# Four shift products of a query block: a turn of four score tiles of their own, or four 32-column tiles beside a block of sums

## Chip, cores and metric

One NeuronCore of a Trainium2 chip. The metric is the device time of one execution in microseconds (us), the median of the runs.

## What is computed

Two rounds of the same two layers on x of 2048 rows by 512 columns, float32. Cut to what matters here (the second layer, a mixer over the rows, is left out):

```python
q = (layernorm(x) @ wq).reshape(1, 2048, 32, 16).transpose(0, 2, 1, 3)
k, v = layernorm(x) @ wk, layernorm(x) @ wv          # one key and value head of 16 for all 32 heads
scores = einsum("bhqd,bkd->bhqk", q, k) * 16 ** -0.5
x = x + (softmax(scores) @ v).transpose(0, 2, 1, 3).reshape(1, 2048, 512) @ wo
```

The kernel takes no maximum of the scores ahead of the exponential. Each query and head gets a shift from a bound: minus 0.515625 times its squared length, times a bound on the keys. It goes into the score product as two more rows. The sums of squares over the 16 columns of a head are the "shift products" of this case.

## The kernel before

**Tiling.** The 2048 queries are four blocks b of 512. A block's 512 query columns are four quarters m of 128 columns (8 heads of 16), and a quarter makes two groups of four heads. So a layer has 32 groups, and a group has 32 score tiles: 16 key tiles by two pairs of heads, 1024 tiles in a layer. `scores` (L906) makes one tile with two matmuls on two halves of the rows into a two-bank PSUM tile `sc` (three of them), and ScalarE writes the exponential to `p` (L922). Some tiles are first copied by VectorE (L920). `sums` (L924) multiplies `p` with values and ones: each float32 product is two matmuls of 32 columns in the trace, and two tiles with j0 = 0 and 2 fill the four 32-column tiles of the array side by side, `acc` (L928). `acc` of a group is one of two PSUM banks, by the group's parity; the other one is the spare bank in which projections are made (`spare`, L946).

**The order of TensorE's work** is written out in turns (L36 to L53), run by `Attention.run` (L988). A positive number k makes k % 10 score tiles (13 means three, the last copied by VectorE), 0 takes the next part (a projection or the like), and a negative number drains so many tiles into sums. The four that matter, with one letter for each:

```python
WHOLE = (13, 0, 0, 13, -4, 13, -4, 13, -4)                  # W, 12 tiles
LONG = (2, 0, 13, -4, 13, -4, 13, 0, 13, -4, 12, -4)        # L, 16 tiles
TINY = (2, 0, 2, -4)                                        # T, 4 tiles
PLAIN = (2, -2)                                             # P, 2 tiles
```

**What is queued.** `Proj.later` (L649) lists the query work that is left when the attention of a layer begins. For a quarter it is a W with two parts of six matmuls, `pq` (L418). After a block's last quarter comes a T with the block's shift products, `shifts` (L548). Layer 0 has 14 quarters and four T, layer 1 has 11 quarters and four T. All must be over before tile 256, and a turn that would cross tile 64 (layer 0), 128 (layer 1) or 256 is replaced by P (L1019 to L1023). A W becomes an L where 14 tiles or more are left in the group being summed and `slack` (L983) is at least 4. That is 256, less the tiles scored, less the sizes of all queued turns, less 48 (before tile 160) or 12. An L doesn't begin with 2, 4 or 32 tiles left in the group, nor a W with 2 (L1026, L1028); a P stands there. Output projections `po` come ahead of the queue once their divisions are done in `mix.step` on VectorE, one or two small steps at a drain. When nothing else is to be had, P follows P up to tile 256.

**A quarter's way.** The second part sets `behind` (L705): at the next drain `put_queries` (L541) rounds `pq` on VectorE (L519), squares it on GpSimd into `sq` (L527), subtracts on VectorE (L531) and stores by SyncE's queue. `shifts` multiplies `sel` (a 0 or -0.515625 matrix, 128 by 32 for each quarter) with `sq` of the four quarters, one after the other into the same 32 PSUM rows (L552). Then VectorE takes the minimum `qmin` (L556) and the copy `c2` (L557), and one DMA writes `c2` (L717). `lowest` (L596) sends `qmin` through DRAM to one row for the check of the bound, `flag` (L611), which the guards at those tiles read. Between the layers `shifts` runs once with two quarters, from L1624. The way in (L1491) makes quarter 0 of layer 0 by itself (L1506).

Of the kernel before, what the change touches and what calls it, by code (L numbers as in the profile page):

```python
# [18 lines left out]
P = 128  # L19
# [30 lines left out]
SHORT = (2, 0, 3, -4, 3, -4)  # L50
TINY = (2, 0, 2, -4)
PLAIN = (2, -2)
# [20 lines left out]
def kernel(  # L73
# [37 lines left out]
    ident = cp.tile([P, P], F32, tag="ident", name="ident")  # L111
    sel = cp.tile([P, ND, H], BF16, tag="sel", name="sel")
    selk = cp.tile([P, 1], BF16, tag="selk", name="selk")
    b1c = cp.tile([P, NF], F32, tag="b1c", name="b1c")
    b2c = cp.tile([P, NKT], F32, tag="b2c", name="b2c")
    qmin = cp.tile([H, NB + 1], F32, tag="qmin", name="qmin")
    k2m = cp.tile([P, NKT], F32, tag="k2m", name="k2m")
# [3 lines left out]
    cd = dp.tile([NB * NG, 4, 2, QB], F32, tag="cd", name="cd")  # L121
    fd = dp.tile([3, H, NB], F32, tag="fd", name="fd")
    hd = [dp.tile([P, ND, 2, QB], F32, tag=f"hd{b}", name=f"hd{b}") for b in range(2)]
# [7 lines left out]
    def f32(ap):  # L131
        return ap.bitcast(F32)
# [6 lines left out]
    def constants():  # L139


        kr = cp.tile([1, 4, P], F32, tag="kr", name="kr")
        half = kr.rearrange("o j (e r) -> o j e r", e=2)
        nc.gpsimd.memset(kr, 0.0)
        nc.gpsimd.memset(kr[:, 1, :], 1.0)
        nc.gpsimd.memset(half[:, 0, :, 2 * R1 + 1 : KR], 1.0)
        nc.gpsimd.memset(half[:, 1, :, 2 * R1 + 1 : KR], -1.0)
        for t in range(3):
            nc.gpsimd.memset(half[:, 2, :, t * R1 : t * R1 + 1], 1.0)
        nc.gpsimd.memset(kr[:, 3, 1:R1], 1.0)  # L150
        pk = bank(0, "pkc")
        for j in range(4):
            nc.tensor.matmul(pk[:, j : j + 1], kr[:, j, :], onerow[:, :1], start=True, stop=True)
        heat(16, bank(1, "pw"))
        nc.gpsimd.memset(vaug[:, :, :, 1], 1.0)
        nc.gpsimd.memset(sel, -SHIFT)
        for m in range(ND):

            nc.gpsimd.affine_select(
                sel[:, m, :], sel[:, m, :], pattern=[[-DH, H]], compare_op=ALU.is_ge,  # L160
                fill=0.0, base=P * m, channel_multiplier=1,
            )
            nc.gpsimd.affine_select(
                sel[:, m, :], sel[:, m, :], pattern=[[DH, H]], compare_op=ALU.is_ge,
                fill=0.0, base=DH - 1 - P * m, channel_multiplier=-1,
            )
        return pk
# [83 lines left out]
    class Proj:  # L251
        def __init__(self, layer, spare=None):
            n = self.l = layer
            self.sq, self.h, self.hT, self.kv, self.y = {}, {}, {}, {}, {}
            self.kk, self.kg, self.pk, self.pq, self.q2, self.st = {}, {}, {}, {}, {}, {}
            self.pt, self.halves = {}, {}

            self.spare, self.half = spare, None
            if spare:
                self.first = pool(f"first{n}", side="right")  # L260

            k = self.keep = pool(f"keep{n}")
            self.wq = k.tile([P, ND, 2, D], F32R, tag="wq", name=f"wq{n}")
            self.c2 = k.tile([H, 2, QB], F32R, tag="c2", name=f"c2_{n}")
            p = self.pool = pool(f"proj{n}")
            self.wkv = p.tile([P, ND * 2, P], F32R, tag="wkv", name=f"wkv{n}")
# [29 lines left out]
        def empty(self, eng=None):  # L296
            nc.vector.memset(f32(self.wkv), 0.0)
            eng = eng or nc.vector
            eng.memset(f32(self.c2), 0.0)
            self.ones = self.pool.tile([P, P], F32, tag="ones", name=f"ones{self.l}")  # L300
            eng.memset(self.ones, -SHIFT)
# [245 lines left out]

        def shifts(self, b, pc=None, parts=range(ND)):  # L548

            pc = (bank2(f"pc{self.l}_{b}")[:, 0, :] if pc is None else pc)[:H, :]  # L550
            for m in parts:
                nc.tensor.matmul(  # L552
                    pc, sel[:, m, :], self.sq.pop((b, m)), start=(m == parts[0]), stop=(m == parts[-1])
                )
            c = b + 1 if b or parts[0] else 0
            nc.vector.tensor_reduce(qmin[:, c : c + 1], pc, axis=AX.X, op=ALU.min)  # L556
            nc.vector.tensor_copy(self.c2[:, 0, :], pc)  # L557
            put_shifts(self.c2, NG * b + 2 * parts[0], NG * b + 2 * parts[-1] + 2, 8 * parts[0])

# [45 lines left out]
        def load_lowest(self, j, k):  # L605

            self.far = sm.tile([1, H, NB - 1], F32, tag="far", bufs=1, name=f"far{self.l}_{j}")
            nc.sync.dma_start(self.far[:, :, :k], fd[j : j + 1, :, :k])
            self.low = k
# [39 lines left out]
        def later(self, att):  # L649

            n, work = self.l, []

# [5 lines left out]

            def rows(b, parts=range(ND)):
                put(TINY, [lambda i: self.shifts(b, bank(i, f"pc{n}_{b}"), parts)])  # L660

            def far(j, lo, hi):
                then(-1, lambda: self.lowest(j, lo, hi))

# [4 lines left out]
            if n == 0:  # L669
                project(0, range(2, ND))  # L670
                then(-1, lambda: (self.first.release(), att.weights()))
                rows(0, range(1, ND))
                far(1, 1, 2)
                for b in range(1, NB):
                    project(b)
                    rows(b)
            else:
                att.weights()
                project(NB - 2, [ND - 1])
                then(-1, lambda: self.fetch(0))  # L680
                rows(NB - 2)
                project(0, range(2, ND))
                then(-1, lambda: (self.fetch(1), att.split_weights(1)))
                rows(0, range(2, ND))
                far(1, 1, 2)
                for b in (NB - 1, 1):
                    project(b)
                    rows(b)
            for j in range(2 - n):
                k = j + (3 if n == 0 else 2)  # L690
                then(k, lambda j=j: att.split_weights(j))
            far(2, 2, NB + 1)
            return work

# [99 lines left out]
    class Attention:  # L794
        def __init__(self, layer):
# [4 lines left out]
            self.spares, self.taken = None, 0  # L800
            self.behind, self.lag, self.pieces = None, LAG, []

# [180 lines left out]
        def slack(self, later):  # L983

            left = 2 * NKT * NG - self.scored - sum(self.size(t) for t, _, _ in later)
            return left - (48 if self.scored < 2 * NKT * 5 else 12)

        def run(self, mix, proj):  # L988
# [10 lines left out]
            while self.scored < total:  # L999
                mix.chores(self)  # L1000
                ahead = min(t for t in guards if t > self.scored)
                known = ahead < guards[-2] or not later
                if ahead < total and self.scored >= ahead - 16 and flagged < ahead and known:
                    flagged = ahead
                    proj.flag(proj.flagged)
                if turn is None:
                    turn = PLAIN
                    self.lag = 2 * LAG if mix.normed and self.scored < total - 16 else LAG
                    if len(self.pend) == self.lag:
                        after, queued = None, bool(later) and not mix.projections  # L1010
                        if queued:
                            turn, parts, after = later[0]
                            if turn is WHOLE and self.to_boundary() >= 14 and self.slack(later) >= 4:
# [17 lines left out]
                for k in turn:  # L1031
                    if k > 0:
                        self.more(mix, k)
                    elif k == 0:
                        if queued and turn is TINY:
                            mix.step(2.0, self)
                        parts.pop(0)(self.spare())
                        if turn is DOUBLE and len(parts) % 2:
                            mix.step(1.0, self)
                        if queued and not parts:  # L1040
                            later.pop(0)
                            if after:
                                after()
                            if not later:
                                proj.close()
                                mix.open()
                    else:
# [4 lines left out]
                        if busy:  # L1052
                            self.behind = None
                            busy()
                        self.drain(-k)
                        mix.chores(self)
# [7 lines left out]
                        elif end:  # L1064
                            mix.step(2.0, self)
                assert self.scored < guards[-2] or not later
                if self.scored in guards[:-1] and self.scored > guarded:
# [423 lines left out]
    def way_in(order, proj):  # L1491
# [13 lines left out]
        def pc():  # L1505
            nc.tensor.matmul(halves("pc", 0)[:H, :], sel[:, 0, :], proj.sq.pop((0, 0)), start=True, stop=True)  # L1506

        def c2():
            nc.scalar.copy(proj.c2[:, 0, :], halves("pc", 0)[:H, :])

        def qmin_():
            nc.vector.tensor_reduce(qmin[:, :1], halves("pc", 0)[:H, :], axis=AX.X, op=ALU.min)

# [213 lines left out]
```

## Time and profile before

| what | value |
|---|---|
| runs | 2510.74, 2510.95, 2515.05 us; median 2510.95 |
| span of the profiled execution | 2509.2 us |
| median less that span (what lies around it) | 1.75 us |
| TensorE busy, granted clock | 2492.8 us, 99%; 0.999 |
| ScalarE, VectorE, GpSimd busy | 2101.7, 1550.9, 148.2 us |

The span runs from the first to the last instruction of the one execution that was profiled; durations below are of it. Starts on TensorE are exact, while ends of matmuls are modelled, so that a block's price is read from its start to the start of the next.

### The profile page before, as it was taken

To read this page: it belongs to the slowest core of one execution; us is meant where nothing else is said; L and a number is where in the kernel's file an instruction comes from. 1 tells how busy PE (TensorE), PEld (TensorE's weight loads), DVE (VectorE), ACT (ScalarE), POOL (GpSimd) and SP (SyncE) were. 2 spreads that over 40 slices of the span, in tenths; PEclk is the share of its full clock that TensorE was granted. 3 is DMA by queue.
4 is the path that set the end of the run, shared out by engine and by line. 5 is a ranking of instruction groups with operands and counts; after the bars stand their busy time and mean duration, and the time that the engine had idled before them with its cause. 6 is when DMAs were issued, how large, how long until landed. Compare 5 with 4: busy or idle time off the path is not lost. (4 is left out here: it accounts for less than half of the span.)

```text
span 2509.2 us, 41946 instructions
## 1 busy us (share of the span) xinstructions
PE 2492.8 (99%) x16158; PEld 1240.5 (49%) x16158; DVE 1550.9 (62%) x2458; ACT 2101.7 (84%) x2344; POOL 148.2 (6%) x235
## 2 busy tenths in 40 slices
PE   8999999999999999999999999999999999999999
PEld 6444344444444444588863443444444444445887
DVE  6566566667766776564445664666677667765522
ACT  6999999999999999653349999999999999995511
POOL 5000000000000000141000000000000000002200
PEclk9999999999999999999999999999999999999999
DMA  3221201111111111144423211111111111102343
GB/s 117 75 66 41 65 28 40 31 42 31 39 31 39 31 40 32 41 112 149 126 61 118 58 48 48 31 39 33 39 31 39 32 43 33 40 26 67 106 125 96
DMA packets 168679, 143.56 MB, mean 57 GB/s; under 512 B 17650, under 2 KB 132368, under 8 KB 167952
## 3 DMA queue, kind: packets, MB, share of 16 engines
q1 hardware_dynamic: 168464, 140.72, 19.0%
q8 instruction: 132, 2.16, 0.4%
q14 instruction: 83, 0.68, 0.1%
HBM read 97.67 MB, written 26.22 MB: 49 GB/s over the span
## 5 line engine op out<-in xcount | busy, mean ns | idle before, releaser
L922 ACT ACTIVATE p<-sc 128x1024 f32<-128x1024 f32 x1444 | 1405.8, 1049 | 62.9 <-PE sc L912 62.2
L920 DVE COPY p<-sc 128x1024 f32<-128x1024 f32 x604 | 739.1, 1224 | 522.3 <-PE sc L912 436.4
L928 PE MATMUL acc<-p,vaug 128*32 128x512 f32 x8192 | 1000.1, 599 | 0.5 <-DVE q L531 0.5
L912 PE MATMUL sc<-qs,kst 51*128 51x512 f32 x4096 | 683.5, 432 | 6.8 <-SPq L630 2.7
L922 ACT ACTIVATE p<-p 128x1024 f32<-128x1024 f32 x604 | 655.9, 1086 | 14.1 <-DVE p L920 9.2
L912 PEld LDWEIGHTS sc<-qs,kst 51*128 51x128 f32 x4096 | 338.3, 184 | 559.5 <-ACT p L922 387.3
L928 PEld LDWEIGHTS acc<-p,vaug 128*32 128x32 f32 x8192 | 219.0, 109 | 489.3 <-issue 472.9
L1458 PE MATMUL py<-u,w 128*128 128x512 f32 x1344 | 307.4, 390 | 0.0
L1458 PEld LDWEIGHTS py<-u,w 128*128 128x128 f32 x1344 | 251.9, 188 | 52.3
L1446 ACT CAST w<-w2r 128x896 fp32r<-128x896 f32 x64 | 60.3, 945 | 184.6 <-PE py L1458 177.3
L1205 PE MATMUL pu<-hb,w 128*128 128x512 f32 x792 | 209.6, 406 | 0.0
L1205 PEld LDWEIGHTS pu<-hb,w 128*128 128x128 f32 x792 | 140.9, 188 | 57.7 <-issue 31.9
L1192 POOL TENSOR_TENSOR w<-w1r,w 128x256 fp32r<-128x256 f32 x86 | 70.0, 822 | 1581.5 <-ACT w L1190 1581.1
L1447 DVE TENSOR_TENSOR w<-w2r,w 128x896 fp32r<-128x896 f32 x64 | 72.0, 1124 | 111.4 <-ACT w L1446 111.2
L848 DVE RECIPROCAL o<-o 128x128 f32<-128x128 f32 x120 | 113.3, 944 | 9.4 <-DMA o<-ev 9.4
L889 PE MATMUL po<-wo,hl 128*128 128x512 f32 x360 | 100.4, 412 | 0.1
L830 DVE COPY ev<-acc 128x512 f32<-128x512 f32 x64 | 43.7, 682 | 62.1 <-PE acc L928 62.1
L418 PE MATMUL pq<-hT,wq 128*128 128x512 f32 x312 | 81.1, 404 | 0.0
L889 PEld LDWEIGHTS po<-wo,hl 128*128 128x128 f32 x360 | 62.6, 188 | 33.9 <-issue 16.0
L1205 PE MATMUL pu_l<-hb,w 128*128 128x512 f32 x336 | 77.1, 389 | 0.0
L1464 DVE SCALAR_TENSOR_TENSOR x<-py,b2c,x 128x512 f32<-128x512 f32 x32 | 24.0, 750 | 81.2 <-PE py L1458 81.2
L1190 ACT CAST w<-w1r 128x256 fp32r<-128x256 f32 x86 | 34.5, 406 | 47.1 <-PE pu_l L1205 14.3
(191 smaller groups left out, 1179.0 us busy)
## 6 DMA issues: line engine op xcount, KB each, us to landing
w1r<-in_B_w_dram SPq DMA_DIRECT2D x224, 128.0 KB
w2r<-in_B_w_dram SPq DMA_DIRECT2D x64, 448.0 KB
qs<-qd SPq DMA_DIRECT2D x384, 64.0 KB
qd<-q SPq DMA_DIRECT2D x64, 256.0 KB
o<-ev SPq DMA_DIRECT2D x128, 128.0 KB
x<-in_A_x_dram SPq DMA_DIRECT2D x16, 256.0 KB
hd<-hT SPq DMA_DIRECT2D x2, 2048.0 KB
out_dram<-x SPq DMA_DIRECT2D x16, 256.0 KB
```

Of the source, the lines that this page charges most:

```text
L418: yield nc.tensor.matmul(out, a, c, start=(k == 0), stop=(k == len(terms) - 1))
L848: nc.vector.reciprocal(o[:, 1, c], o[:, 1, c])
L889: nc.tensor.matmul(po, a, c, start=(k == 0), stop=(k == 3 * len(parts) - 1))
L912: nc.tensor.matmul(sc[:, j, :], kst[kt // 4][rows, kt % 4 * P : (kt % 4 + 1) * P], qs[i % NQ][rows, j0 // 2, :], start=True, stop=True,)
L920: nc.vector.tensor_copy(pt, sc)
L922: nc.scalar.activation(pt, sc, AF.Exp, scale=0.25)
L928: nc.tensor.matmul(self.acc[i][c : c + 32, :], vaug[:, kt].rearrange("p d k -> p (d k)"), pt[:, j, :], start=(kt == 0), stop=(kt == NKT - ...
L1192: eng.tensor_tensor(w[:, 1], raw, f32(w[:, 0]), op=ALU.subtract)
L1205: nc.tensor.matmul(pu, a, c, start=(start and k == 0), stop=(stop and k == 5))
L1446: nc.scalar.copy(w[:, 0], raw)
L1447: nc.vector.tensor_tensor(w[:, 1], raw, f32(w[:, 0]), op=ALU.subtract)
L1458: nc.tensor.matmul(py, a, d, start=(c == 0 and f == 0 and k == 0), stop=(c == 1 and f == NFH - 1 and k == 2),)
```

## The change

The four products go to four 32-column tiles of one bank: `pc` rows 32m to 32m+31 for quarter m, each a product by itself, with one `sel` for all. `qmin` and `c2` therefore have 128 rows, and each quarter's shifts go out by a DMA of its own. T is gone. What it held is a "tail" of the queue's entry before it, emitted just ahead of a drain once that entry has no part left, if the drain isn't the one that emits `put_queries` and doesn't cross the group's end. Until a tail is out no further turn is taken from the queue. Layer 0's first tail makes quarter 0 again (its `sq` is kept). The core of the diff:

```diff
-TINY = (2, 0, 2, -4)
-    sel = cp.tile([P, ND, H], BF16, tag="sel", name="sel")
+    sel = cp.tile([P, H], BF16, tag="sel", name="sel")
-    qmin = cp.tile([H, NB + 1], F32, tag="qmin", name="qmin")
+    qmin = cp.tile([P, NB + 1], F32, tag="qmin", name="qmin")
-    fd = dp.tile([3, H, NB], F32, tag="fd", name="fd")
+    fd = dp.tile([3, P, NB], F32, tag="fd", name="fd")
...
             eng.memset(f32(self.c2), 0.0)
+            eng.memset(qmin, 0.0)
...
+        def shifts(self, b, pc=None, parts=range(ND), new=0):
+
+            pc = bank2(f"pc{self.l}_{b}")[:, 0, :] if pc is None else pc
             for m in parts:
                 nc.tensor.matmul(
-                    pc, sel[:, m, :], self.sq.pop((b, m)), start=(m == parts[0]), stop=(m == parts[-1])
+                    pc[H * m : H * m + H, :], sel, self.sq.pop((b, m)), start=True, stop=True,
+                    skip_group_check=True,
                 )
-            put_shifts(self.c2, NG * b + 2 * parts[0], NG * b + 2 * parts[-1] + 2, 8 * parts[0])
+            rows = slice(H * parts[0], H * parts[-1] + H)
+            c = b + 1 if b or ND - 1 in parts else 0
+            nc.vector.tensor_reduce(qmin[rows, c : c + 1], pc[rows, :], axis=AX.X, op=ALU.min)
+            nc.vector.tensor_copy(self.c2[rows, 0, :], pc[rows, :])
+            for m in parts[new:]:
+                put_shifts(self.c2, NG * b + 2 * m, NG * b + 2 * m + 2, H * m)
...
-            def rows(b, parts=range(ND)):
-                put(TINY, [lambda i: self.shifts(b, bank(i, f"pc{n}_{b}"), parts)])
+            def rows(b, parts=range(ND), new=0):
+                tails[len(work) - 1] = [lambda i: self.shifts(b, bank(i, f"pc{n}_{b}"), parts, new)]
...
-                        if queued and turn is TINY:
-                            mix.step(2.0, self)
...
+                        elif self.tail and not parts and self.to_boundary() >= -k > 0:
+                            spare = self.spare()
+                            for part in self.tail:
+                                part(spare)
+                            self.tail = None
+                            if not later:
+                                proj.close()
+                                mix.open()
                         self.drain(-k)
```

In the way in, `sel` takes two `affine_select` on GpSimd in place of eight. The row that `lowest` loads takes 8 of each quarter's 32 rows of `fd`.

## Rows read from the trace of the kernel before

**Rows 1.** The page, part 1: busy us, share of the span, instructions.
```profile
PE 2492.8 (99%) x16158; PEld 1240.5 (49%) x16158; DVE 1550.9 (62%) x2458; ACT 2101.7 (84%) x2344; POOL 148.2 (6%) x235
```
**Rows 2.** Windows: stretch, then busy us of PE, PEld, DVE, ACT, POOL; clock, DMA.
```profile
57.00:291.00 234.00, 233.18 (x1617) 99.05 (x1609) 136.63 (x176) 219.28 (x235) 14.56 (x14) 1.00 0.22 59
...
1527.00:1545.00 18.00, 18.00 (x120) 5.65 (x118) 2.78 (x11) 18.00 (x21) 0.00 (x0) 1.00 0.18 52
```
**Rows 3.** Timeline of PE, a W and a T of layer 0: start us, us, what.
```profile
136.50 0.96 PE L912 MATMUL sc<-qs,kst 51*128 51x512 f32 x6
...
143.09 0.96 PE L912 MATMUL sc<-qs,kst 51*128 51x512 f32 x6
143.98 1.92 PE L928 MATMUL acc<-p,vaug 128*32 128x512 f32 x16
...
148.58 0.73 PE L912 MATMUL sc<-qs,kst 51*128 51x512 f32 x4
149.25 1.04 PE L552 MATMUL pc<-sq,sel 128*32 128x512 bf16 x4
150.22 0.95 PE L912 MATMUL sc<-qs,kst 51*128 51x512 f32 x4
...
152.95 0.97 PE L912 MATMUL sc<-qs,kst 51*128 51x512 f32 x6
```
**Rows 4.** Timeline of PE, the first T of layer 0 (three products).
```profile
86.17 0.73 PE L912 MATMUL sc<-qs,kst 51*128 51x512 f32 x4
86.83 0.82 PE L552 MATMUL pc<-sq,sel 128*32 128x512 bf16 x3
87.58 0.88 PE L912 MATMUL sc<-qs,kst 51*128 51x512 f32 x4
...
90.25 0.73 PE L912 MATMUL sc<-qs,kst 51*128 51x512 f32 x4
```
**Rows 5.** Timeline of PE in layer 1: an L and the T behind it.
```profile
1308.99 0.73 PE L912 MATMUL sc<-qs,kst 51*128 51x512 f32 x4
...
1322.64 1.92 PE L928 MATMUL acc<-p,vaug 128*32 128x512 f32 x16
1324.50 0.73 PE L912 MATMUL sc<-qs,kst 51*128 51x512 f32 x4
...
1328.65 0.73 PE L912 MATMUL sc<-qs,kst 51*128 51x512 f32 x4
```
**Rows 6.** Timeline of PE in layer 1: the last T, the first P behind it and a later one.
```profile
1520.88 0.73 PE L912 MATMUL sc<-qs,kst 51*128 51x512 f32 x4
...
1525.13 0.73 PE L912 MATMUL sc<-qs,kst 51*128 51x512 f32 x4
...
1526.79 0.73 PE L912 MATMUL sc<-qs,kst 51*128 51x512 f32 x4
...
1530.54 0.73 PE L912 MATMUL sc<-qs,kst 51*128 51x512 f32 x4
...
1532.37 0.73 PE L912 MATMUL sc<-qs,kst 51*128 51x512 f32 x4
```
**Rows 7.** Timelines of DVE and POOL behind the pq of Rows 3.
```profile
142.59 0.68 DVE L519 CAST q<-pq 128x512 fp32r<-128x512 f32 x1
...
143.41 1.04 POOL L527 TENSOR_TENSOR sq<-q 128x512 bf16<-128x512 f32 x1 [11.07 <-DVE q L519]
```
**Rows 8.** Timeline of POOL behind the pq of Rows 5.
```profile
1322.20 1.04 POOL L527 TENSOR_TENSOR sq<-q 128x512 bf16<-128x512 f32 x1 [21.96 <-DVE q L519]
```
**Rows 9.** Tile pc, the minimum: engine, operation, count, ns min/median/max, first and last start.
```profile
L556 DVE TENSOR_REDUCE qmin<-pc x9: 669/679/679, 87.7 to 1523.9; 32x1 f32<-32x512 f32 x9
```
**Rows 10.** Timeline of SP behind the last T of layer 0.
```profile
288.20 0.34 SPq L717 DMA_DIRECT2D cd<-c  x1
```
**Rows 11.** Timelines of PE and POOL in the way in.
```profile
3.23 1.86 PE L153 MATMUL pkc<-onerow,kr 1*128 1x1 f32 x8 [3.23 <-POOL kr L146]
...
7.44 0.46 POOL L311 TENSOR_TENSOR wkvhl<-wkvr,wkvhl 128x128 fp32r<-128x128 f32 x1 [1.74 <-DVE mv_a L339]
```

More of the change, by code (lines that the diff above doesn't have):

```diff
@@ L156, in constants @@
         nc.gpsimd.memset(sel, -SHIFT)
[L157 to L166, printed above, removed]
+        nc.gpsimd.affine_select(
+            sel, sel, pattern=[[-DH, H]], compare_op=ALU.is_ge, fill=0.0, base=0, channel_multiplier=1
+        )
+        nc.gpsimd.affine_select(
+            sel, sel, pattern=[[DH, H]], compare_op=ALU.is_ge, fill=0.0, base=DH - 1, channel_multiplier=-1
+        )
         return pk
@@ L263, in __init__ @@
             self.wq = k.tile([P, ND, 2, D], F32R, tag="wq", name=f"wq{n}")
-            self.c2 = k.tile([H, 2, QB], F32R, tag="c2", name=f"c2_{n}")
+            self.c2 = k.tile([P, 2, QB], F32R, tag="c2", name=f"c2_{n}")
             p = self.pool = pool(f"proj{n}")
@@ L546, in put_queries @@
             self.store_queries(b, m)
-        def shifts(self, b, pc=None, parts=range(ND)):
-            pc = (bank2(f"pc{self.l}_{b}")[:, 0, :] if pc is None else pc)[:H, :]
+        def shifts(self, b, pc=None, parts=range(ND), new=0):
+            pc = bank2(f"pc{self.l}_{b}")[:, 0, :] if pc is None else pc
             for m in parts:
                 nc.tensor.matmul(
-                    pc, sel[:, m, :], self.sq.pop((b, m)), start=(m == parts[0]), stop=(m == parts[-1])
-                )
-            c = b + 1 if b or parts[0] else 0
-            nc.vector.tensor_reduce(qmin[:, c : c + 1], pc, axis=AX.X, op=ALU.min)
-            nc.vector.tensor_copy(self.c2[:, 0, :], pc)
-            put_shifts(self.c2, NG * b + 2 * parts[0], NG * b + 2 * parts[-1] + 2, 8 * parts[0])
+                    pc[H * m : H * m + H, :], sel, self.sq.pop((b, m)), start=True, stop=True,
+                    skip_group_check=True,
+                )
+            rows = slice(H * parts[0], H * parts[-1] + H)
[4 more added lines that the diff above has]
+                put_shifts(self.c2, NG * b + 2 * m, NG * b + 2 * m + 2, H * m)
         def first_bound(self, blocks):
@@ L607, in load_lowest @@
             self.far = sm.tile([1, H, NB - 1], F32, tag="far", bufs=1, name=f"far{self.l}_{j}")
-            nc.sync.dma_start(self.far[:, :, :k], fd[j : j + 1, :, :k])
+            rows = fd[j : j + 1].rearrange("o (m r) k -> o m r k", m=ND)[:, :, : H // ND, :k]
+            nc.sync.dma_start(self.far[:, :, :k].rearrange("o (m r) k -> o m r k", m=ND), rows)
             self.low = k
@@ L649, in later @@
         def later(self, att):
-            n, work = self.l, []
+            n, work, tails = self.l, [], {}
             def put(turn, parts):
@@ L657, in then @@
                 work[k] = (*work[k][:2], after)
-            def rows(b, parts=range(ND)):
-                put(TINY, [lambda i: self.shifts(b, bank(i, f"pc{n}_{b}"), parts)])
+            def rows(b, parts=range(ND), new=0):
+                tails[len(work) - 1] = [lambda i: self.shifts(b, bank(i, f"pc{n}_{b}"), parts, new)]
             def far(j, lo, hi):
-                then(-1, lambda: self.lowest(j, lo, hi))
+                tails[len(work) - 1].append(lambda i: self.lowest(j, lo, hi))
             def project(b, parts=range(ND)):
@@ L671, in later @@
                 then(-1, lambda: (self.first.release(), att.weights()))
-                rows(0, range(1, ND))
+                rows(0, range(ND), 1)
                 far(1, 1, 2)
@@ L689, in later @@
             for j in range(2 - n):
-                k = j + (3 if n == 0 else 2)
+                k = j + (2 if n == 0 else 1)
                 then(k, lambda j=j: att.split_weights(j))
             far(2, 2, NB + 1)
-            return work
+            return [(*entry, tails.get(k)) for k, entry in enumerate(work)]
         def in_halves(self, att, b, m):
@@ L800, in __init__ @@
             self.spares, self.taken = None, 0
-            self.behind, self.lag, self.pieces = None, LAG, []
+            self.behind, self.lag, self.pieces, self.tail = None, LAG, [], None
         def weights(self):
@@ L983, in slack @@
         def slack(self, later):
-            left = 2 * NKT * NG - self.scored - sum(self.size(t) for t, _, _ in later)
+            left = 2 * NKT * NG - self.scored - sum(self.size(entry[0]) for entry in later)
             return left - (48 if self.scored < 2 * NKT * 5 else 12)
@@ L1001, in run @@
                 ahead = min(t for t in guards if t > self.scored)
-                known = ahead < guards[-2] or not later
+                known = ahead < guards[-2] or not (later or self.tail)
                 if ahead < total and self.scored >= ahead - 16 and flagged < ahead and known:
@@ L1009, in run @@
                     if len(self.pend) == self.lag:
-                        after, queued = None, bool(later) and not mix.projections
-                        if queued:
-                            turn, parts, after = later[0]
+                        after, queued = None, bool(later) and not mix.projections and not self.tail
+                        if self.tail:
+                            turn, parts = PLAIN, []
+                        elif queued:
+                            turn, parts, after, tail = later[0]
                             if turn is WHOLE and self.to_boundary() >= 14 and self.slack(later) >= 4:
@@ L1041, in run @@
                             later.pop(0)
+                            self.tail = tail
                             if after:
                                 after()
-                            if not later:
-                                proj.close()
-                                mix.open()
                     else:
@@ L1065, in run @@
                             mix.step(2.0, self)
-                assert self.scored < guards[-2] or not later
+                assert self.scored < guards[-2] or not (later or self.tail)
                 if self.scored in guards[:-1] and self.scored > guarded:
@@ L1505, in pc @@
         def pc():
-            nc.tensor.matmul(halves("pc", 0)[:H, :], sel[:, 0, :], proj.sq.pop((0, 0)), start=True, stop=True)
+            nc.tensor.matmul(halves("pc", 0)[:H, :], sel, proj.sq[0, 0], start=True, stop=True)
         def c2():
-            nc.scalar.copy(proj.c2[:, 0, :], halves("pc", 0)[:H, :])
+            nc.scalar.copy(proj.c2[:H, 0, :], halves("pc", 0)[:H, :])
         def qmin_():
-            nc.vector.tensor_reduce(qmin[:, :1], halves("pc", 0)[:H, :], axis=AX.X, op=ALU.min)
+            nc.vector.tensor_reduce(qmin[:H, :1], halves("pc", 0)[:H, :], axis=AX.X, op=ALU.min)
         def pq():
```

## Prediction

> **What bounds the kernel now.** I began with the page: TensorE is busy for 99% of the span, ScalarE for 84% [rows 1]. Such a share is modelled, so I took the windows next. In layer 0's stretch of queued query work TensorE is full (233.18 of 234 us), and ScalarE nearly so (219.28, 94%) [rows 2]. Which of them sets the pace is read from the timeline of TensorE, by starts. In a W three score tiles take 0.89 us (143.09 to 143.98) and the whole turn 12.08 us (136.50 to 148.58) [rows 3]. An L takes 15.51 (1308.99 to 1324.50) [rows 5]. These prices are the same wherever they occur, so nothing is waited for: in W and L TensorE sets the pace, 1.007 and 0.969 us a tile. In a run of P it is ScalarE: the window between 1527 and 1545 has it busy for all 18.00 us [rows 2], and there a P takes 1.83 us (1530.54 to 1532.37), while the first one behind a T, for which nothing is late yet, takes 1.66 (1525.13 to 1526.79) [rows 6]. So a us saved on TensorE counts in W, L and T, and nothing in a run of P.
>
> **What goes.** Eight T. Those shown take 4.37 (148.58 to 152.95) [rows 3], 4.08 [rows 4], 4.15 (1324.50 to 1328.65) [rows 5] and 4.25 [rows 6], mean 4.21, so eight are 33.7 us. In one, the four products one after the other are 0.97 us (149.25 to 150.22) [rows 3]; three are 0.75 [rows 4], so one more product costs 0.22 and 0.09 is fixed. The rest of a T is score tiles and sums, and those don't go: they have to be done in other turns.
>
> **Where the 32 tiles land.** I followed the queue's rules turn by turn from tile 12 to 256. Without the T, `slack` is larger, so some W become L, and what is left becomes P.
>
> - Layer 0 before: 2 L, 12 W, 4 T, 10 P. After: L at tile 12, W at 28 with the first tail, L at 40, five P around the guard at 64 and one more at the group's start, L at 68 and 84; from 100 on the slack is 0, so W at 100, 112, 124, 136, 148, two P at 160, the two L of output projections as before, W at 196, 208, 220, 232, six P. That is 4 L, 10 W, 14 P. Check: 4 x 16 + 10 x 12 + 14 x 2 = 212 = 2 x 16 + 12 x 12 + 4 x 4 + 10 x 2.
> - Layer 1 before: 9 L, 2 W, 4 T, 14 P. After: L 12, W 28, L 40, W 56, L 68, 84, 100, W 116, two P, L 132, 148, 164, then the projections and 22 P: 8 L, 3 W, 24 P, 212 again.
>
> Tile 256 is reached in the same state, so the order behind it stays.
>
> Layer 0: two W turn into L, 2 x (15.51 - 12.08) = 6.86; four P more, 4 x 1.83 = 7.32; four T less, 16.84: **-2.66**. Layer 1: one L turns into W, -3.43; ten P, 18.30; -16.84: **-1.97**. Together -4.63 us. I take a P at 1.83 as in a run, since most of them stand in the runs ahead of tile 256 (6 and 22); at TensorE's own 1.66 [rows 6] the 14 more P would be 14 x 0.17 = 2.4 us cheaper.
>
> **The products in their new place.** Beside the sums the products fill four column tiles at once. No row shows bf16 products side by side. The sums are nearest: 16 matmuls of as many columns in four column tiles last 1.86 us (1322.64 to 1324.50), 0.12 each [rows 5], where a product in one column tile costs 0.22 [rows 4]. The bounds are nothing and one after the other, 0.97; I take one product's 0.22 for all four, as the sums lie side by side: 8 x 0.22 = **+1.76** (bounds 0 and +7.8).
>
> The Trainium skill, "TensorE: Matmul & The Clock Gate", Part 3, measured 2.38 times for three column tiles, not 3. By that share an estimate for four products is 0.28, and the sum would be 0.5 us higher. No run here shows it yet.
>
> **The new wait.** In a T a turn's rest lay between a block's last `pq` and its products; now one drain does. A tail may not go to the drain that emits `put_queries`, so it goes to the next. In a W that is the drain at 143.98 [rows 3], but the last quarter's rounding ends at 143.27 and its square on GpSimd at 144.45 [rows 7]. So the fourth product is 0.47 us late. In an L the drain is at 1322.64 [rows 5] and the square ends at 1323.24 [rows 8], 0.60 late. Behind the waiting product stand the four tiles of sums and all later scores; the other three products are made meanwhile. From rounding to GpSimd 0.14 us pass [rows 7], so I add 0.1 for the release. The first tail of layer 0 escapes: at its second drain (30 tiles summed) two are left in the group, so it goes to the third, 2.7 us later. The others do not: three W in layer 0, four L in layer 1 (one with two products), 3 x 0.57 + 4 x 0.70 = **+4.5** (bounds 0, if sums pass the waiting product, and +7.3, if the square's whole 1.04 us [rows 7] is waited for seven times).
>
> The same page of the Trainium skill says, in Part 3, that matmuls keep strict program order and only weight loads are pulled ahead. By that rule the wait counts in full, as above; without it the sum would be 4.5 lower. The trace agrees as far as it goes: no block here starts ahead of the one emitted before it.
>
> **What costs nothing.** VectorE's minimum, 0.68 us [rows 9], and the copy of the same form were in T; they read as many columns from 128 rows as from 32. With 0.7 of wait and 0.4 for the product they are over 2.5 us after the drain begins. The bank's next writer, a `pq` or a group's first sums, comes after the sums (1.86 and the wait) and a block of scores (0.9), at 3.5; with that cover gone it would wait for VectorE, 0.7 at most. SyncE's queue issues 24 DMAs more at 0.34 [rows 10], 8 us over 450, ahead of loads that are wanted a group (30 us) later. The checks of the bound get `qmin` as early, against tiles 64, 128 and 256. Between the layers two products side by side save **-0.2**. In the way in, the six `affine_select` that go leave no gain, as GpSimd waits 1.74 us behind them [rows 11]. The memset of `qmin` comes ahead of the row for which TensorE waits at 3.23 [rows 11], **+0.1**. A store of 128 tiny rows may delay the first check, 0 to +0.4.
>
> **Sum.** -4.63 + 1.76 + 4.5 - 0.2 + 0.1 = +1.5 us on a span of 2509.2, so the median goes from 2510.95, which is 1.75 above that span, to **2512.5**. A measurement tells about 0.2%, 5 us, from no change.
>
> **The rivals.**
> - *The wait is not paid.* The square comes in time, or the sums pass it. For: GpSimd is idle otherwise. Against: [rows 3, 7] and [rows 5, 8] give its end behind the drain each time. It gives 1.5 - 4.5 = -3.0, 2508.0. Chance 0.20.
> - *TensorE alone counts.* The wait is not paid, and P after P costs 1.66, since the freed time lets ScalarE run ahead. Against: ScalarE's 18.00 of 18.00 [rows 2]. -3.0 - 2.4 = -5.4, 2505.6. Chance 0.08.
> - *Slower: the products do not lie side by side,* because bf16 products and float32 sums of one column layout don't share the array or each has to load its weights by itself. At 0.97 in place of 0.22 it is 8 x 0.75 = 6 more, +7.5 us, 2518.5. It decides from 0.66 us for four products on (1.5 + 8 x 0.44 = 5). For: no row shows bf16 so. Against: the sums do it throughout. Chance 0.12.
> - *It does not do what it says:* tails find no drain and go later, behind a P. Then the wait is gone, but later quarters are held up by P turns: about 0, 2511. Chance 0.06.
>
> **How the numbers follow.** The forecast has 0.54. The range leaves out the case of TensorE alone and most of the slower one: from 2507.5, below the case without the wait, to 2517, which takes in the forecast's upper bounds for the wait and the P. Faster by over 0.2%: 0.08 and a little of the first rival, 0.10. Slower by over 0.2%: 0.12 and a little of the forecast's upper end, 0.13. Within 0.2%: 0.77.
>
> **What would show it.** In the profile after, TensorE's timeline must show L552 right ahead of L928, seven times with some 0.6 us between the third product and the fourth, and the wait named as POOL's `sq`; a drain with four products of 2.1 us where nothing is waited for; 14 P more, 22 in one run ahead of tile 256 in layer 1. If the idle time ahead of the fourth product is missing, the wait step is wrong; if a drain with products takes over 2.5 us without it, the side-by-side step is; if the turns differ in number, my reading of the queue is.

## The result, and the profile after

The changed kernel takes 2514.61 us, median of 21 runs (2511.69 to 2518.49), against 2510.97 of before (21 runs, 2510.25 to 2515.05). The ratio is 1.0013 [1.0007, 1.0019]: slower by 3.3 us (1.8 to 4.8), where +1.5 was forecast. Taken again later with other kernels it gave 1.0013 [1.0004, 1.0022].

The page's head of the changed kernel, to hold against [rows 1]:

```profile
span 2510.0 us, 41971 instructions
...
PE 2490.7 (99%) x16159; PEld 1241.9 (49%) x16159; DVE 1552.1 (62%) x2460; ACT 2101.3 (84%) x2344; POOL 147.3 (6%) x230
```

Nothing in it tells of the loss, and its span is only 0.8 us longer. The kernels share an order of work outside the query stretch, so I cut there: from the score tile numbered 12, where the queue begins, to the one numbered 256, where it must be empty. First the timeline of TensorE before (layer 1's start stands in [rows 5]):

```profile
58.29 0.50 PE L912 MATMUL sc<-qs,kst 51*128 51x512 f32 x2
...
302.89 0.68 PE L912 MATMUL sc<-qs,kst 51*128 51x512 f32 x2 [0.78 <-DMA qs<-qd]
...
1547.89 0.67 PE L912 MATMUL sc<-qs,kst 51*128 51x512 f32 x2 [0.78 <-DMA qs<-qd]
```

The same four tiles in the changed kernel:

```profile
58.02 0.50 PE L912 MATMUL sc<-qs,kst 51*128 51x512 f32 x2
...
301.89 0.68 PE L912 MATMUL sc<-qs,kst 51*128 51x512 f32 x2 [0.78 <-ACT p L922]
...
1306.94 0.73 PE L912 MATMUL sc<-qs,kst 51*128 51x512 f32 x4
...
1549.35 0.67 PE L912 MATMUL sc<-qs,kst 51*128 51x512 f32 x2 [0.78 <-DMA qs<-qd]
```

Layer 0's stretch went from 244.60 to 243.87 us (-0.73), layer 1's from 238.90 to 242.41 (+3.51). The whole loss is in layer 1. The spans differ by less than the two stretches together (+2.78), since the rest of the changed execution came out shorter: 0.27 us ahead of layer 0's stretch, 1.05 between the two, 0.66 behind layer 1's. In the part between them the profiled execution before had one more stretch at the lower of the clock's two levels, 1.2 GHz, just ahead of layer 1's queue. Windows from 1298.6 to 1302.0, the clock is the number before the DMA share; before, then changed:

```profile
1298.60:1302.00 3.40, 3.40 (x16) 1.09 (x15) 3.29 (x6) 2.75 (x3) 1.04 (x1) 0.51 0.67 144
```

```profile
1298.60:1302.00 3.40, 3.25 (x24) 1.10 (x24) 3.28 (x8) 3.40 (x5) 0.49 (x1) 1.00 0.92 245
```

That stretch stands in some executions of either kernel, so one profile's total is a poor measure here, and the cut stretches and the medians are used. Runs of equal mean granted clock show the loss too: in the later measurement the changed kernel's median is 2514.08 us at a clock of 0.999 (3 runs) and 2514.36 at 0.998 (5), where the kernel before has 2510.38 (11) and 2511.49 (11).

**The tails.** Timeline of TensorE, changed kernel: the first tail (no wait), a tail in a W, the first in layer 1 (in an L). L548 are the products.

```profile
83.83 0.40 PE L548 MATMUL pc<-sq,sel 128*32 128x512 bf16 x4
84.06 1.91 PE L928 MATMUL acc<-p,vaug 128*32 128x512 f32 x16
85.90 0.73 PE L912 MATMUL sc<-qs,kst 51*128 51x512 f32 x4
...
150.89 0.96 PE L912 MATMUL sc<-qs,kst 51*128 51x512 f32 x6
151.82 0.83 PE L548 MATMUL pc<-sq,sel 128*32 128x512 bf16 x4
152.28 2.09 PE L928 MATMUL acc<-p,vaug 128*32 128x512 f32 x16
154.30 0.96 PE L912 MATMUL sc<-qs,kst 51*128 51x512 f32 x6
...
1319.90 0.74 PE L912 MATMUL sc<-qs,kst 51*128 51x512 f32 x4
1320.83 0.77 PE L548 MATMUL pc<-sq,sel 128*32 128x512 bf16 x4 [0.20 <-DVE q L527]
1321.22 2.09 PE L928 MATMUL acc<-p,vaug 128*32 128x512 f32 x16
1323.24 0.97 PE L912 MATMUL sc<-qs,kst 51*128 51x512 f32 x6
1325.93 1.39 PE L414 MATMUL pq<-hT_0r,wq 128*128 128x512 f32 x5 [1.71 <-DMA hT_0r<-hd]
```

Without a wait the products take 0.23 us to the first sums, and a drain with them takes 2.07 (83.83 to 85.90), 0.21 over a drain alone. In the W the sums start 0.46 behind the first product: a narrower cut of the same timeline shows the fourth product at 152.28 by itself, and GpSimd's square ends at 151.19 + 1.04 = 152.23:

```profile
152.28 0.38 PE L548 MATMUL pc<-sq,sel 128*32 128x512 bf16 x1
```

```profile
151.19 1.04 POOL L523 TENSOR_TENSOR sq<-q 128x512 bf16<-128x512 f32 x1 [8.10 <-DVE q L515]
```

The drain with products lasts 2.48 us (151.82 to 154.30), 0.63 over one alone, and the scores ahead 0.03 more. In the L the products come 0.93 behind the scores' start (0.66 elsewhere), as the bank is first let go by VectorE's L527, and the drain lasts 2.41, together 0.83 more. The other tails of layer 1 take 0.90, and the wait for L527 is in all four. It lies within the wait for the square: in this first one GpSimd's square ends at 1321.17, past the 1320.83 at which the bank was free.

**What the forecast did not have** stands in the last line of that fence. (That row is cut by the window's end: the `pq` has twelve matmuls.) The W behind the first tail reads `hT_0r`, a block of 2 MB that comes back from DRAM, and TensorE sits idle for 1.71 us. The load is issued when the first quarter's matmuls have let its buffer go. Issues by SyncE's queue, changed and before, and the first use before (tile `hT_0r`; the times are of the first and last start):

```profile
1317.29 0.35 SPq L647 DMA_DIRECT2D hT_0r<-hd  x1
```

```profile
1319.37 0.35 SPq L647 DMA_DIRECT2D hT_0r<-hd  x1
```

```profile
L418 PE MATMUL pq<-hT_0r,wq x24: 388/395/505, 1332.9 to 1357.6; 128*128 128x512 f32 x24
```

Before, 13.5 us lay between the issue and the first use. They held the T and two P. Now it would be 6.9, and the load takes 8.6.

### The profile page after: what moved, and what is told of

Its sections match the earlier page's. It is cut to its first block, busy times and chain, and to the rows that moved or that the text cites. A ratio compares the mean times of both kernels' runs of the same rounds, so it can differ in the third digit from the quotient of the medians.

```text
span 2510.0 us, 41971 instructions
## 1 busy us (share of the span) xinstructions
PE 2490.7 (99%) x16159; PEld 1241.9 (49%) x16159; DVE 1552.1 (62%) x2460; ACT 2101.3 (84%) x2344; POOL 147.3 (6%) x230
```

## Experiments

All kernels are measured against the one before on the same chip. There its median was 2510.97 us for "T kept", "two P", "one drain later" and "in a row", 2511.23 for "changed, again", "load in halves" and the two with later tails and P, and 2512.38 for the last. The stretches are cut at tiles 12 and 256 as above, in the profiled execution. An interval of 0.0009 to either side is 2.3 us, so few of the ratios tell a kernel from the one before; the changed kernel's stretches, taken twice, agree within 0.17 us, and the causes are read from them.

| kernel | layer 0, us | layer 1, us | median, us | ratio to before |
|---|---|---|---|---|
| before | 244.60 | 238.90 | 2510.97 | |
| changed | 243.87 | 242.41 | 2514.61 | 1.0013 [1.0007, 1.0019] |
| changed, again | 243.70 | 242.27 | 2514.36 | 1.0013 [1.0004, 1.0022] |
| side by side, T kept | 244.29 | 238.54 | 2511.80 | 1.0001 [0.9992, 1.0010] |
| two P ahead of the load's reader | 243.68 | 238.75 | 2511.16 | 0.9995 [0.9986, 1.0004] |
| load in halves | 243.82 | 240.56 | 2512.07 | 1.0000 [0.9991, 1.0009] |
| tail one drain later | 244.95 | 238.37 | 2513.38 | 1.0003 [0.9994, 1.0012] |
| products in a row | 245.17 | 244.83 | 2516.35 | 1.0016 [1.0007, 1.0025] |
| later tails and two P | 242.79 | 242.85 | 2514.32 | 1.0009 [1.0000, 1.0018] |
| and P spread | 243.50 | 241.01 | 2513.05 | 1.0001 [0.9992, 1.0011] |
| halves and later tails | 242.86 | 238.24 | 2510.25 | 0.9990 [0.9981, 0.9999] |

**1. The load: is it the missing loss?** Theory: yes. Rival: the products or the turns cost more than reckoned. First, two P put ahead of the reader:

```diff
                             later.pop(0)
                             self.tail = tail
+                            if self.l == 1 and len(later) == 10:
+                                plains = 2
...
                             turn, parts = PLAIN, []
+                        elif plains:
+                            turn, parts, queued, plains = PLAIN, [], False, plains - 1
```

> The changed kernel with two P in layer 1 behind the first quarter, ahead of the W whose projection reads the block loaded again from DRAM (hT_0r); two P fewer stand in the run ahead of tile 256. Main theory (the change took away the 8 us of turns that hid that load, and the 1.7 us of idle time ahead of pq hT_0r in the profile is more in most runs): the idle time goes to 0, the profile's stretch falls by 1.7 to 2 us, the runs' spread from 2511.7 to 2518.5 shrinks to that of before, the median goes to 2510 to 2512. Rival (the spread is from elsewhere): at most 1.7 us off the median, spread as wide.

The idle time is gone and the median is 2511.16 (2508.20 to 2513.29). Layer 1 is 3.66 us shorter, more than the wait, since the P also move the turns behind them: two of its four tails no longer wait for the square. So the second way leaves the order alone. The first eight products of a `pq` need only the high halves of the block:

```diff
-            nc.sync.dma_start(f32(self.hT[b]), hd[b])
+            for j in range(2):
+                nc.sync.dma_start(f32(self.hT[b][:, :, j, :]), hd[b][:, :, j, :])
```

> The changed kernel, the order of all turns as it is; only the load hT_0r (and hT_1r) comes in two DMAs, the high halves first, for which the first eight products of the pq are enough. Main theory (the wait for that load is the loss that the forecast missed): the idle time ahead of pq hT_0r falls from 1.7 us to under 0.3, the stretch from tile 12 to 256 of layer 1 falls by 1.5 to 2, the median by 2 to 4 (with the half clock that follows the wait in some runs): 2511 to 2513. Rival (the load is hidden anyway or the spread has another cause): 0.5 or less.

The timeline of TensorE there has no idle time ahead of the `pq`:

```profile
1323.78 0.98 PE L913 MATMUL sc<-qs,kst 51*128 51x512 f32 x6
1324.69 3.12 PE L414 MATMUL pq<-hT_0r,wq 128*128 128x512 f32 x12
```

Layer 1 fell by 1.85 us, layer 0 stayed, the median fell by 2.3 to 2.5 us and the runs end at 2514.46 where the changed kernel's end at 2518.83. That is as expected by the theory, and the rival falls: the load is 1.7 to 1.9 us of the loss in the profile (against the two profiles of the changed kernel), and about 2.4 in the median, which is good to some 2 us. Run for comparison, the changed kernel again:

> The changed kernel once more, on the chip of the next three. Main theory: about 2514.6, 3 to 4 us over before; the profile has 1 to 3 us of idle time ahead of pq hT_0r, and where a stretch of half clock follows it, some 2 us more. Rival (the difference to before was the chip or the day): within 1 us of before.

It had 1.6 us of idle time there, and no lower clock behind it.

**2. The square: does the fourth product's wait cost its full length?** A tail goes one drain later:

```diff
+                        elif self.tail and not parts and self.late:
+                            self.late -= 1
                         elif self.tail and not parts and self.to_boundary() >= -k > 0:
...
-                            self.tail = tail
+                            self.tail, self.late = tail, 1
```

> The changed kernel with every tail one drain later (in a W the third drain; behind an L a P, which then isn't in the run ahead of tile 256). Main theory (the fourth product waits for its square, 3 times 0.45 us in layer 0 and 4 times 0.68 in layer 1, and all sums behind it with it): 4 us less, a drain with products takes 2.06 us everywhere; the P behind the first L also hides 1.2 of the 1.7 us for hT_0r; 5 us under the changed kernel, 2509 to 2510. Rival (the sums and the scores behind make the wait good, ScalarE sets the pace): 1 us or less.

The wait is gone: a W's drain now begins with

```profile
155.81 0.40 PE L548 MATMUL pc<-sq,sel 128*32 128x512 bf16 x4
156.04 1.89 PE L928 MATMUL acc<-p,vaug 128*32 128x512 f32 x16
157.86 0.96 PE L912 MATMUL sc<-qs,kst 51*128 51x512 f32 x6
```

0.23 and 2.05 us. Layer 1 fell by 4.04, the 2.7 of its four waits and most of the load's (0.25 us of it is left). Yet the median is only 1 us lower, because layer 0 lost at its end and behind it: the part between the two stretches, too, is 3.9 us longer than before (1010.0 and 1006.1), with 6.8 us at the lower clock at either end of it. Layer 0's last tail now stands in the last drain ahead of the run of P to tile 256. The row of `qmin` comes 3.3 us later, and the guard's read on SyncE's queue, behind loads that wait for VectorE, which waits for that row, is late. The loads of that row, in the changed kernel and here:

```profile
291.38 0.72 SPq L608 DMA_DIRECT2D far<-fd  x1
```

```profile
294.70 0.72 SPq L608 DMA_DIRECT2D far<-fd  x1
```

What TensorE then does:

```profile
299.64 1.24 PE L928 MATMUL acc<-p,vaug 128*32 128x512 f32 x8
304.29 1.42 PE L912 MATMUL sc<-qs,kst 51*128 51x512 f32 x4 [3.41 <-SPq L630]
```

The window from 1.5 us before the wait's end on, with its granted clock ahead of the DMA share:

```profile
302.80:309.60 6.80, 5.31 (x24) 1.65 (x24) 0.69 (x1) 3.14 (x4) 0.00 (x0) 0.50 0.21 61
```

TensorE idles for 3.41 us, and that window has a granted clock of 0.50, 1.2 GHz. So the theory on the wait holds and the expectation for the whole missed: a third piece of work hangs on the place of the products, the guard's check, and the changed kernel's place still hid it.

**3. The products: does their place beside the sums matter?** The changed order, but the four one after the other into 32 rows as before:

```diff
-                    pc[H * m : H * m + H, :], sel, self.sq.pop((b, m)), start=True, stop=True,
-                    skip_group_check=True,
+                    pc, sel[:, m, :], self.sq.pop((b, m)), start=(m == parts[0]), stop=(m == parts[-1])
```

> The changed order, but the products one after the other into the same 32 rows, as before the change. Main theory: the first three, 0.65 us, are made while the fourth waits, so in the seven tails that wait the place of the products hardly matters: 0.3 us each in a W, 0.05 to 0.2 in an L, and 0.7 in the one that doesn't wait, together 1.5 to 2.5 us over the changed kernel. Rival (side by side is what the changed order lives on): 8 x 0.65 = 5 us over it.

1.7 to 2.0 us over the changed kernel by medians, so within the expectation, but medians alone are too coarse for it. The drains tell: those with products last 0.41 us longer in the tail that doesn't wait (three products here), 0.21 in each W and 0.28, 0, 0.21 and 0.21 in the four L, 1.7 together and far from the rival's 5. The rest of layer 1's longer stretch is the load's wait and the lower clock behind it. In a W the fourth product begins 0.66 us behind the first and the next scores come 2.69 behind it (2.48 side by side):

```profile
152.27 0.82 PE L551 MATMUL pc<-sq,sel 128*32 128x512 bf16 x3
152.74 0.63 PE L927 MATMUL acc<-p,vaug 128*32 128x512 f32 x3
152.93 0.38 PE L551 MATMUL pc<-sq,sel 128*32 128x512 bf16 x1
153.15 1.88 PE L927 MATMUL acc<-p,vaug 128*32 128x512 f32 x13
154.96 0.96 PE L911 MATMUL sc<-qs,kst 51*128 51x512 f32 x6
```

Two products are made and the third begins (152.71) by the time the fourth's square ends (151.64 + 1.04 = 152.68), so side by side hardly shortens a tail that waits. And the products in a row don't keep the whole array from the sums: three sums start at 152.74, ahead of the fourth product, which stands ahead of them in the program. What the fourth still waited for must be its own column tile, busy with the third; that the three sums are those of the other column tiles fits their number, but the trace doesn't name the tiles. This execution also shows what the load's wait can bring behind it, the `pq` at 1.2 GHz, 4.51 us (1327.97 to 1332.48) in place of 2.93 in the changed kernel (1325.93 to 1328.86):

```profile
1327.97 4.57 PE L417 MATMUL pq<-hT_0r,wq 128*128 128x512 f32 x12 [1.85 <-DMA hT_0r<-hd]
1332.48 0.73 PE L911 MATMUL sc<-qs,kst 51*128 51x512 f32 x4
```

The window behind the wait, with its granted clock ahead of the DMA share:

```profile
1328.80:1332.20 3.40, 3.40 (x10) 2.52 (x8) 0.00 (x0) 0.00 (x0) 0.00 (x0) 0.50 0.03 7
```

**4. The products alone, T kept.** The changed kernel with its T back:

```diff
+TINY = (2, 0, 2, -4)
...
-                tails[len(work) - 1] = [lambda i: self.shifts(b, bank(i, f"pc{n}_{b}"), parts, new)]
+                put(TINY, [lambda i: self.shifts(b, bank(i, f"pc{n}_{b}"), parts, new)])
...
+                        if queued and turn is TINY:
+                            mix.step(2.0, self)
...
-                        elif self.tail and not parts and self.to_boundary() >= -k > 0:
...
```

> The side-by-side products alone: the turn T of four score tiles stays as before, only its products go to four column tiles. Main theory (the products side by side cost 0.22 in place of 0.97 us, and what the change loses is lost by the products' new place in the order): each T falls from 4.2 to about 3.5 us on TensorE, 8 x 0.65 = 5 us; ScalarE gets 3.7 us of work in a T, so some of it is given back: 2 to 5 us faster than before, 2506 to 2509. Rival (side by side brings nothing, the fixed part of a block of its own eats it): within 1 us of before.

The same as before within the interval (0.8 us by medians): the expectation missed, and the rival's number held. The T at layer 0's second block:

```profile
149.01 0.73 PE L913 MATMUL sc<-qs,kst 51*128 51x512 f32 x4
149.68 0.40 PE L549 MATMUL pc<-sq,sel 128*32 128x512 bf16 x4
150.01 0.49 PE L913 MATMUL sc<-qs,kst 51*128 51x512 f32 x2
151.09 0.50 PE L913 MATMUL sc<-qs,kst 51*128 51x512 f32 x2 [0.59 <-ACT p L923]
...
153.37 0.97 PE L913 MATMUL sc<-qs,kst 51*128 51x512 f32 x6
```

The products fell from 0.97 to 0.33 us, and the second of the two score tiles behind them now waits for ScalarE to free a `sc`: it starts 1.08 behind the first. The T lasts 4.36 us, as long as before (4.37 [rows 3]); all eight together are 0.6 us shorter, and the two stretches 0.7. A T makes four score tiles with three `sc` and no sums between, so its middle goes at ScalarE's pace, and the products in a row were mostly hidden there.

**5. Which version beats both?** Later tails where no guard follows at once, and two P for the load:

```diff
-                            self.tail = tail
+                            if self.l == 1 and len(later) == 10:
+                                plains = 2
+                            self.tail, self.late = tail, 1 if later or self.l else 0
```

> The changed kernel with every tail one drain later but for the last of layer 0 (whose check the guard at tile 256 waits for), and two P ahead of the first read of hT_0r. Main theory (waits for the square 0.45 in two W and 0.68 in four L, the load 1.7, and what half clock follows): layer 0 from tile 12 to 256 is 1.5 us shorter than before the change, layer 1 1 to 2; median 2508 to 2510, under both kernels. Rival (the waits' time comes back behind them): 2512 or more.

A miss: layer 0 is 1.81 us shorter than before, as expected, but in layer 1 the two P and the later drain together put a tail into the last drain ahead of the guard at tile 128. SyncE's queue stands at the tail's DMAs, which wait for `c2`, and the guard's read is behind them:

```profile
1420.96 1.64 SPq L717 DMA_DIRECT2D cd<-c  x4
```

```profile
1419.12 0.40 PE L548 MATMUL pc<-sq,sel 128*32 128x512 bf16 x4
1419.35 1.89 PE L928 MATMUL acc<-p,vaug 128*32 128x512 f32 x16
1424.78 1.42 PE L912 MATMUL sc<-qs,kst 51*128 51x512 f32 x4 [3.54 <-SPq L630]
```

The window behind the wait, with its granted clock ahead of the DMA share:

```profile
1424.90:1431.70 6.80, 6.80 (x28) 1.95 (x28) 0.69 (x1) 3.88 (x4) 0.00 (x0) 0.50 0.34 101
```

Again an idle TensorE (3.54 us) and a clock of 0.50 behind it. With one P behind every queued turn of layer 1 besides (`plains = 2 if len(later) == 10 else 1`):

> The kernel of the run before with one P behind every queued turn of layer 1, so that about ten P leave the run ahead of tile 256. Main theory (a P in a run goes at ScalarE's 1.83 us, one between turns in which TensorE sets the pace at 1.66): 1.5 to 2 us under the run before. Rival (ScalarE's work is the same wherever the tile stands and the following turns pay for it): the same as the run before within 0.5.

Layer 1 was 1.84 us shorter and the median 1.3, but the turns and guards shifted again, with up to 1.9 us of idle time at one of them, so whether a P costs less between other turns isn't told by it. The last one takes the load in halves (as in 1) and later tails but for layer 0's last, without extra P:

```diff
-                            self.tail = tail
+                            self.tail, self.late = tail, 1 if later or self.l else 0
```

> The kernel with the load in halves, and every tail one drain later but for the last of layer 0, so that no tail stands in the last drains ahead of a guard. Main theory (three separate waits: the fourth product's square, 0.45 us in two W and 0.68 in four L; the load, 1.7; a guard that comes right behind a tail and finds SyncE's queue still at the tail's DMAs, 2.4 to 3.4 us and half clock behind it): all three are gone, layer 0 from tile 12 to 256 is 1.5 us and layer 1 1.3 us shorter than before the change, median 2508.5 to 2510.5, 3 us or more under the changed kernel and 0.5 to 2.5 under the kernel before. Rival (the waits' time comes back elsewhere, as where late tails met the guards): 2512 or more.

2510.25 us (2508.45 to 2511.59) against 2512.38 of the kernel before measured beside it (15 runs), 0.9990 [0.9981, 0.9999]: some 4 us under the changed kernel's medians, and under before by an interval that only just leaves out no change. Six of those 15 runs of before have a mean granted clock of 0.997 and take 2514.18 us or more; the median of the other nine is 2510.51, only 0.3 over the 2510.25 here. So the medians alone don't show that it beats before. The stretches say more: layer 0 is 1.74 and layer 1 0.66 us shorter than before. And against the load in halves alone, from which this kernel differs only in the later tails, they are 0.96 and 2.32 shorter, where two waits of 0.45 and four of 0.68 were taken away. A W's tail there:

```profile
156.72 0.40 PE L548 MATMUL pc<-sq,sel 128*32 128x512 bf16 x4
156.94 1.89 PE L929 MATMUL acc<-p,vaug 128*32 128x512 f32 x16
158.76 0.96 PE L913 MATMUL sc<-qs,kst 51*128 51x512 f32 x6
```

## Why the prediction was right, and where it was not

The forecast was no change within 0.2%, on the slow side, 2512.5 in 2507.5 to 2517.0. The measured 2514.61 lies in that range, and +0.13% lies within 0.2%.

- **The turns** came as reckoned. The queued turns, and the P between them, stand in the trace where the count put them: products at 40, 109, 157 and 241 tiles scored in layer 0, at 28, 56, 116 and 180 in layer 1, and 22 P in one run ahead of tile 256.
- **The products** cost 0.21 us where 0.22 was taken (1.86 to 2.07). The rival that they would not lie side by side falls: without a wait four take 0.23 to the first sums. The share that the Trainium skill, "TensorE: Matmul & The Clock Gate", Part 3, gives for three column tiles made the estimate 0.28. The measurement decides, and no loss shows.
- **The wait** for the square is there in seven of eight tails, as said. Wait and product together cost 0.66 in a W (0.57 + 0.22 = 0.79 was taken) and 0.83 to 0.90 in an L (0.92). The fourth product began 0.38 to 0.46 behind the third where some 0.6 was named as the sign; in the L the rest of the lateness went by ahead of the first product, in the wait for the bank. The sums didn't pass the product that waits for its square. The Trainium skill, "TensorE: Matmul & The Clock Gate", Part 3, states a strict order of matmuls. These waits agree with it, but the starts in experiment 3 don't: there three sums start ahead of a product whose square is ready. Against the rivals in which the wait isn't paid, taking it away shortened both stretches (the last kernel of experiment 5 against the load in halves).
- **The step that failed** is "What costs nothing": it went through VectorE, SyncE's issues (of the shifts 22 more, not 24) and the checks, and left out the load that `later` hangs on the first quarter of layer 1 (`self.fetch(0)`). The T and two P hid it. The result is 2.1 us over the forecast; the load is 1.8 in the profile and 2.4 in the median. Without it (the load in halves) the two stretches are together 0.88 us longer than before, where +1.5 was forecast for the whole. So by the stretches the side, slower, came from terms that were reckoned, and the missing term was small enough for the wide range. With the load layer 1's stretch should have grown by 1.71 + 1.8 = 3.5, and it grew by 3.51 (the forecast's own 1.71 is -1.97 + 4 x 0.22 + 2.80). Layer 0's should have stayed (-2.66 + 0.88 + 1.71 = -0.07) and fell by 0.73: of the 0.66 between, 0.4 is the three W tails (0.66 each, not 0.79), and where the other 0.26 came from was not separated.
- **A sentence that was wrong** without harm to the sum is that a us saved on TensorE counts in a T. Experiment 4 shows that ScalarE sets the pace in its middle. The sum used whole turns, so it held.
- **The run of P** at ScalarE's pace held: 1.83 us each in the changed kernel too.

Open: how the loss beyond the cut stretches varies. The changed kernel's runs spread over 7 and 8 us, those with the load in halves over 4; but the kernel before, in 33 runs, spreads over 6.5 by itself. One execution of the changed order with the products in a row shows the lower clock behind the load's wait; the two profiles of the changed kernel do not. In how many runs it comes is not known: of a run without a profile there is only the mean granted clock.

## What to carry to other kernels

When a piece of work is moved or removed, list what stood under it: every load issued ahead of it and first used behind it, every flag or guard that is read a fixed number of turns later. Here the removed turn cost more by itself than what replaced it, but it hid a 2 MB load and a square on GpSimd, and both came out; once the products went later still, so did a trip of the check through DRAM. Put a product as late as the next reader of its result allows, not beside the first work of its own shape; and take a saving on one engine as such only where the profile shows that no other one sets the pace of that very turn.

## What was not expected of the hardware

- Four bf16 products in four column tiles run side by side, and float32 sums follow them with no cost for the change of type that shows: 0.23 us from the first product to the first sums, and 1.84 for those sums, where they take 1.86 alone.
- A product that waits for its square holds back the sums behind it (0.38 to 0.46 us in seven tails). One whose square is ready, and whose column tile is still busy, doesn't hold back all of them: in experiment 3 three sums start 0.19 us ahead of it (152.74 and 152.93).
- An idle time of TensorE can cost more than itself: with 3.41, 3.54 and, in one execution, 1.85 us of it came a granted clock of 0.50 (1.2 GHz), and a P took 3.21 us (1424.78 to 1427.99) in place of 1.66 to 1.83. Behind 1.71 and 1.6 us of idle time at the place of the 1.85 it stayed at 1.00. The length of the idle time alone doesn't decide: at layer 1's first guard TensorE idles for 1.51 to 1.65 us in all eleven profiles, and the clock falls to 0.50 behind it in seven of them, the one of before (below) among them. Behind 1.92 us (the run with P spread, 1549.80 to 1551.72) it stayed at 1.00.

```profile
1298.32 1.75 PE L912 MATMUL sc<-qs,kst 51*128 51x512 f32 x6 [1.51 <-SPq L630]
```

- The 2 MB load was 8.6 us from its issue to its first use (1317.29 to 1325.93).
